# One written order for all five engines, and attention dealt out on a plan of 28 ticks a unit

## The chip, the cores and the metric

The kernel runs on one core of a Trainium2 chip. Time is device microseconds (us) of one execution, and lower is better. The core has five engines, each with a queue of its own: PE (matmul, with PEld for its weight loads), DVE (vector), ACT (activation), POOL (GpSimd) and SP (which issues most DMAs). An engine starts its instructions in the order in which they stand in its queue; an instruction whose input is not ready, or whose output buffer is still in use, holds up all that stand behind it.

## The reference

A block of a transformer with 2048 tokens of width 448: the input, plus a causal attention in four segments with a carried memory, plus a gated feed-forward.

```python
xn = _layernorm(x, axis=-1)
return x + _A_ref(xn, ...) + _B_ref(xn, ...)
# _A_ref: 16 heads of 28, four segments of 512 tokens
logits = jnp.einsum("bhqd,bhkd->bhqk", qs, ks) * scale + mask
p = _softmax(logits, axis=-1)
a_dot = jnp.einsum("bhqk,bhkd->bhqd", p, vs)
o = g * a_mem + (1.0 - g) * a_dot      # a_mem: phi(q) on the memory of the earlier segments
...
# _B_ref: 448 -> 1792 twice, and back
h = _sigmoid(g) * u
return jnp.einsum("bsf,fd->bsd", h, w_down)
```

## The kernel before, in words

**Precision.** Operands are split into a high part (a rounded fp32r copy, made by ACT) and a low part (the remainder, made by DVE). A product is the sum of three partial products, so that one 128x512 result of the feed-forward takes 11 matmuls (`TERMS`), and a projection back six.

**Front.** The first 150 us or so: layer norm, transposes, queries, keys, values and the segment memories. It stands under a schedule of its own (`FRONT`) and the change does not touch it.

**Loop.** Then two streams share the engines.

- *Feed-forward* (`gated`): for each pair of 128-wide slices f, and each of four token blocks b, four slots. A slot is one run of 11 matmuls into `pgu`: side 0 (gate) into a bank tagged `gu`, side 1 (up) into a bank tagged `p`. After side 1, ACT takes tanh of the gate side (`sg`, "the tanh copy"), DVE multiplies it with the up side, ACT makes the high half of `hh`, DVE the low half. Each slot also takes one item off a list of `down` products: six matmuls into `pd`, and an addition to `acc` by DVE. `pd` of odd t shares the two `gu` banks with the gate side, so that two consecutive gate sides get the same bank: **the next gate run on PE cannot start before the tanh copy of the one before it**. New weights (`wgu`, `wdn`, later `wo`) are split by ACT and DVE at fixed slots (`ahead`).
- *Attention*: 32 pairs of heads, two pairs to a unit, 16 units. A pair has five scores (`st`, two PSUM banks tagged `s`), each copied to `w` by ACT and masked by POOL (`affine_select`). Three of them are followed by a maximum on DVE (`mx`). The maxima are joined in short steps that go between DVE and POOL (`up`, `top`), spread by a DVE transpose (`mb`), and then in three parts subtracted from `w` on DVE and put through Exp on ACT. When both pairs of a unit are done, 32 small matmuls form `pa` ("the sums"), and DVE transposes, divides and transposes back, and POOL stores the result to `od`.

**What sets the order.** The code yields at many points. The loop at the end advances attention by one step whenever the feed-forward's steps have gone far enough (n_att attention steps in all, spread evenly between `LEAD` and `TAIL`). Before, attention has 14 steps to a unit (`SLOT`): a score in 10 of them, the sums of the previous unit in step 7, and the later stages of a pair queued one per step behind its scores (`PARTS`). Only PE and SP keep the order of the source (`MANUAL`); on ACT, DVE and POOL the compiler's list scheduler chooses an order from its own cost estimates.

**Tail.** After the feed-forward, `project` splits the attention results (`sums`, loaded from `od`) into `xs`, high by ACT and low by DVE, and multiplies with `wo` (11 matmuls into `po`, 16 times), while the last `down` products are worked off.

The lines of the steps that follow are: `pgu` L247, tanh copy L255, product L256, `hh` L258 and L259, `pd` L173 and L174, weight splits L85 and L86, score L612, its copy L616 and L619, mask L627, maxima L629 and L633, joins L643 to L653, `mb` L656, subtraction L666, Exp L667, sums L687, `xs` splits L753, L102 and L103, `po` L771. In the changed kernel they are L249, L257, L258, L261 and L264, L175 and L177, L87 and L88, L621, L625 and L628, L636, L643 and L647, L656 to L668, L671, L685, L689, L707, L786, L104 and L105, L804.

Of the kernel before, what the change touches and what calls it, by code (L numbers as in the profile page):

```python
# [9 lines left out]
F32 = mybir.dt.float32  # L10
F32R = mybir.dt.float32r
AF = mybir.ActivationFunctionType
ALU = mybir.AluOpType
# [48 lines left out]
def kernel(  # L62
# [103 lines left out]
    def gated():  # L166

        def down(b, hs, wd, t, tag="pd"):
            tok = slice(t * P, (t + 1) * P)
            mms = [(h[:, a, tok], wd[f][:, w, :]) for f, h in hs for a, w in ((0, 0), (0, 1), (1, 0))]  # L170
            pd = bank("pd", tag)
            for n, (l, r) in enumerate(mms):
                T.matmul(pd[:, :D], l, r, start=n == 0, stop=n == len(mms) - 1)  # L173
            V.tensor_add(acc[b][:, t, :], pd[:, :D], acc[b][:, t, :])  # L174
            yield  # L175
            yield

        raw_up, raw_down, wgu, wdn = {}, {}, {}, {}
# [37 lines left out]
        for f0 in range(0, NF, FG):  # L216
# [22 lines left out]
            for b in range(NB):  # L239
                hs = []  # L240
                for f in range(f0, f0 + FG):
                    pgu = []
                    for side in range(2):
                        slot = 2 * (f - f0) + side
                        dst = bank("pgu", ("gu", "p")[side])
                        for n, (a, w) in enumerate(TERMS):
                            T.matmul(dst, wgu[f][:, w, side * P:(side + 1) * P], xs[b][:, a, :],  # L247
                                     start=n == 0, stop=n == len(TERMS) - 1)
                            if n in (3, 7) and f0 + b == 0:  # L249
                                yield  # L250
                        pgu.append(dst)
                        if side == 1:

                            sg = two_k("sg")
                            A.activation(sg, pgu[0], AF.Tanh, scale=0.5)  # L255
                            V.scalar_tensor_tensor(sg, sg, 1.0, pgu[1], op0=ALU.add, op1=ALU.mult)  # L256
                            hh = four_k(F32R, "hh")  # L257
                            A.activation(hh[:, 0, :], sg, AF.Copy, scale=0.5)  # L258
                            V.scalar_tensor_tensor(hh[:, 1, :], sg, 0.5, hh[:, 0, :].bitcast(F32),  # L259
                                                   op0=ALU.mult, op1=ALU.subtract)  # L260
# [322 lines left out]
    class Pair:  # L583
# [16 lines left out]
            at = HW * h + KB[kb]  # L600
            return self.w[:, at:at + w]

        def scores(self):

            self.w = sb.tile([P, 2 * HW], F32, name="w", bufs=3)
            w3 = self.w.rearrange("p (h n) -> p h n", h=2)
            mx = sb.tile([P, 80], F32, name="mx", bufs=2)
            for n in range(5):
                st = bank("st", "s")
                for h, kb in (((n // 2, 0),), ((n // 2, 1), (n // 2, 3)))[n % 2] if n < 4 else ((0, 2), (1, 2)):  # L610
                    at = KB[kb] % L + (256 * h if kb == 2 else 0)
                    T.matmul(st[:, at:at + L - kb * P], self.qk[:KS, 1, h, kb * P:(kb + 1) * P],  # L612
                             self.qk[:KS, 0, h, kb * P:], start=True, stop=True)
                if n < 4:
                    w = self.w[:, HW * (n // 2) + L * (n % 2):][:, :L]
                    A.activation(w, st, AF.Copy)  # L616
                else:
                    w = w3[:, :, 2 * L:]
                    A.activation(w, st.rearrange("p (h n) -> p h n", h=2), AF.Copy)  # L619

                if n % 2 == 0 and n < 4:  # L621
                    d = w[:, :P]
                    pattern = [[1, P]]
                else:
                    d = w.rearrange("p (a n) -> p a n", n=P)[:, 0:4:3, :] if n < 4 else w[:, :, :P]  # L625
                    pattern = [[0, 2], [1, P]]
                G.affine_select(d, d, pattern=pattern, base=0, channel_multiplier=-1, compare_op=ALU.is_ge, fill=MASK)  # L627
                if n in (1, 3):  # L628
                    V.tensor_reduce(mx[:, 16 * (n - 1):16 * (n + 1)],  # L629
                                    w3[:, n // 2, :2 * L].rearrange("p (b n) -> p b n", n=32),  # L630
                                    axis=mybir.AxisListType.X, op=ALU.max, apply_transpose=True)
                if n == 4:
                    V.tensor_reduce(mx[:, 64:80].rearrange("p (h b) -> p h b", h=2),  # L633
                                    w.rearrange("p h (b n) -> p h b n", n=32),
                                    axis=mybir.AxisListType.X, op=ALU.max, apply_transpose=True)
                yield  # L636
            yield from self.weights(mx)

        def weights(self, mx):

            m = mx[:, :64].rearrange("p (h n) -> p h n", h=2)
            m0 = m[:, :, 0:16]
            V.tensor_max(m0[:, :, 4:16], m0[:, :, 4:16], m[:, :, 16:28])  # L643
            V.tensor_max(m0[:, :, 12:16], m0[:, :, 12:16], m[:, :, 28:32])
            V.tensor_max(m0[:, :, 8:16], m0[:, :, 8:16], mx[:, 64:80].rearrange("p (h n) -> p h n", h=2))
            up = sb.tile([P, 2, 16], F32, name="up")
            top = sb.tile([P, 2, 16], F32, name="top")  # L647
            G.tensor_copy(up[0:64], m0[64:128])
            V.tensor_max(m0[0:64], m0[0:64], up[0:64])
            G.tensor_copy(up[0:32], m0[32:64])  # L650
            V.tensor_max(top[0:32], m0[0:32], up[0:32])
            G.tensor_copy(top[32:64], top[0:32])
            G.tensor_copy(top[64:128], top[0:64])  # L653
            yield
            mb = sb.tile([P, 2, L], F32, name="mb")
            V.transpose(mb.rearrange("p h (b n) -> p (h b) n", n=32),  # L656
                        top.rearrange("p h b -> p (h b)").unsqueeze(2).to_broadcast([P, 32, 32]))
            yield
# [3 lines left out]
            quarters = mb.rearrange("p h (b n) -> p h b n", n=P)  # L662
            for w, m in ((w3[:, :, :L], mb),
                         (rest[:, :, :, P:], mb[:, :, 2 * P:].unsqueeze(2).to_broadcast([P, 2, 2, 2 * P])),
                         (rest[:, :, :, :P], quarters[:, :, 1::2, :])):
                V.tensor_sub(w, w, m)  # L666
                A.activation(w, w, AF.Exp, scale=SCALE)  # L667
                yield  # L668

    class Unit:  # L670

# [8 lines left out]

        def finish(self):

            s, i = self.s, self.i
            pa = bank("pa", "m")
            for kb in range(NT):  # L685
                for j in range(HG):
                    T.matmul(pa[32 * j:32 * j + 32, kb * P:], self.vv[:, kb, 32 * j:32 * j + 32],  # L687
                             self.pairs[j // 2].block(j % 2, kb), start=kb == 0, stop=kb == NT - 1)
            on, oc = (self.pairs[1].w[:, n * L:(n + 1) * L] for n in range(2))  # L689
            V.transpose(on, pa)  # L690
            yield
            weigh(sb, on, gate_n[:, i:i + 1], 0.0)
            V.transpose(oc, on)
            nc.gpsimd.dma_start(od[s][P * i:P * (i + 1)], oc, accum_op=ALU.add if s > 0 else ALU.bypass)
            yield
# [4 lines left out]
    def attention():  # L700
# [1 line left out]
            pairs[n].load()  # L702
        units[0].load_values()
        yield
        run, behind, fin = {}, [], None
        for u in range(len(units) + 1):
            for n in range(2):  # L707
                run[n] = pairs[2 * u + n].scores() if u < len(units) else iter(())
            for k, which in enumerate(SLOT):
                if u == len(units):  # L710

                    if k > 9:
                        break
                    which = ((None,) * 8 + (2, None))[k]
                if behind:
                    next(behind.pop(0))
                if fin:
                    next(fin)
                    fin = None
                if which is not None and which < 2 and u < len(units):  # L720
                    next(run[which])
                    n = 2 * u + which + 2
                    if which not in SLOT[k + 1:]:
                        behind += [run[which]] * PARTS
                        if n < len(pairs):
                            pairs[n].load()
                        else:
                            load_sums(n - len(pairs))
                if which == 2 and u > 0:
                    fin = units[u - 1].finish()  # L730
                    next(fin)
                    if u < len(units):
                        units[u].load_values()
                yield

    sums = {}

# [100 lines left out]
```

## Time and profile before

| | |
|---|---|
| median of 3 runs | 687.23 us (687.1 to 687.6) |
| the profiled execution | 687.17 us, span 685.5 us |
| PE busy | 680.3 us, 99% of the span |
| PEld busy | 566.1 us, 83% |
| DVE busy | 567.1 us, 83% |
| ACT busy | 341.6 us, 50% |
| POOL busy | 146.6 us, 21% |
| granted PE clock | 1.00 in every stretch of 50 us |

The span leaves out 1.67 us that lie around it. The prediction shows the lines that carry its argument. In a timeline the columns are start, length, engine, line, operation, out<-in, shapes and count, and in brackets the idle time before it and what ended it. The length of the last matmul of a row is modelled, so rows overlap; the difference of two starts is what a row really took. "84x384 f32 x2" is a short score of 384 and 128 columns; "84x256 f32 x2" has twice 256. In a list of groups the columns are count, busy time and the mean of one in ns, and the idle time before it.

### The profile page before, as it was taken

The numbers are of one execution on the slowest core, as the hardware profiler recorded it, in microseconds if no ns is written. First come the engines' busy times: TensorE is split into PE (matmuls) and PEld (weight loads), VectorE is DVE, ScalarE is ACT, GpSimd is POOL, SyncE is SP. The second block draws the span as 40 slices with busy tenths as digits, with TensorE's granted clock in tenths as the row PEclk, the third lists the DMA queues.
The fourth block names the chain that finished last, engine by engine and source line by source line (L and its number), as shares of the span: only waits on it lengthen the run. The fifth ranks groups of instructions, "written<-read, shape, count | busy, mean of one in ns | idle before, by whom it ended". The sixth has DMA issues, their size and how long they took to land.

```text
span 685.5 us, 10454 instructions
## 1 busy us (share of the span) xinstructions
PE 680.3 (99%) x3594; PEld 566.1 (83%) x3594; DVE 567.1 (83%) x995; ACT 341.6 (50%) x563; POOL 146.6 (21%) x349
## 2 busy tenths in 40 slices
PE   8999999999999999999999999999999999999998
PEld 7898878778878787887878778787887878778897
DVE  6765695767789998988998889988998899889863
ACT  4837555343554455544556446455643465446220
POOL 3500010101223232222232222222322313212000
PEclk9999999999999999999999999999999999999999
DMA  7446556697232333243324243324342423423352
GB/s 268 178 153 232 205 205 245 244 336 182 71 95 76 95 88 86 57 126 80 90 59 107 62 126 72 99 57 117 81 99 73 97 56 83 94 77 96 92 156 107
DMA packets 45940, 84.37 MB, mean 123 GB/s; under 512 B 6336, under 2 KB 20544, under 8 KB 45376
## 3 DMA queue, kind: packets, MB, share of 16 engines
q1 hardware_dynamic: 42736, 76.26, 36.2%
q0 software_dynamic: 3008, 7.34, 5.1%
q8 instruction: 28, 0.46, 0.3%
q14 instruction: 24, 0.20, 0.1%
q10 hardware_dynamic: 144, 0.11, 0.0%
HBM read 51.05 MB, written 32.64 MB: 122 GB/s over the span
## 4 chain that ended last, share of the span: by engine, by line
PE 96%; DMA 1%; SPq 1%; DVE 1%; issue 0%; ACT 0%; DVEq 0%; ACTq 0%
PE pgu L247 41%; PE pd L173 20%; PE pp L355 10%; PE st L612 6%; PE po L771 5%; PE pa L687 5%; PE pv L335 5%; PE pmm L383 2%; PE n L401 2%; DMA acc<-in_x 1%; SPq L747 1%; PE pt L95 1%; PE pk L375 1%; DMA vv<-vd 0%; DVE stats L294 0%
## 5 line engine op out<-in xcount | busy, mean ns | idle before, releaser
L247 PE MATMUL pgu<-xs,wgu 128*128 128x512 f32 x1232 | 303.6, 393 | 0.0
L247 PEld LDWEIGHTS pgu<-xs,wgu 128*128 128x128 f32 x1232 | 228.2, 188 | 46.9 <-issue 2.4
L173 PE MATMUL pd<-wdn,hh 128*128 128x448 f32 x672 | 155.9, 367 | 0.0
L173 PEld LDWEIGHTS pd<-wdn,hh 128*128 128x128 f32 x672 | 122.4, 188 | 12.0 <-issue 0.8
L627 POOL TENSOR_SCALAR_AFFINE_SELECT w<-w 128x256 f32<-128x256 f32 (+1 forms) x160 | 79.7, 501 | 242.0 <-ACT w L616 193.1
L667 ACT ACTIVATE w<-w 128x1024 f32<-128x1024 f32 (+1 forms) x96 | 87.3, 915 | 87.3 <-DVE w L666 86.8
L666 DVE TENSOR_TENSOR w<-w,mb 128x1024 f32<-128x1024 f32 (+1 forms) x96 | 98.7, 1036 | 0.2
L616 ACT ACTIVATE w<-st 128x512 f32<-128x512 f32 x128 | 74.6, 590 | 43.5 <-PE st L612 43.2
L629 DVE TRANSPOSE_TENSOR_REDUCE mx<-w 128x32 f32<-128x1024 f32 x64 | 78.8, 1231 | 14.9 <-POOL w L627 14.9
L355 PE MATMUL pp<-xs,wqk 128*128 128x512 f32 x308 | 77.7, 401 | 0.0
L174 DVE TENSOR_TENSOR acc<-pd,acc 128x448 f32<-128x448 f32 x112 | 67.2, 600 | 1.1 <-PE pd L173 1.1
L355 PEld LDWEIGHTS pp<-xs,wqk 128*128 128x128 f32 x308 | 56.8, 188 | 13.4 <-issue 2.4
L612 PE MATMUL st<-qk 84*128 84x128 f32 (+3 forms) x256 | 62.2, 312 | 0.1
L258 ACT ACTIVATE hh<-sg 128x512 fp32r<-128x512 f32 x56 | 35.2, 628 | 52.5 <-DVE sg L256 41.9
L612 PEld LDWEIGHTS st<-qk 84*128 84x128 f32 x256 | 47.6, 189 | 7.4 <-ACT w L616 0.6
L255 ACT ACTIVATE sg<-pgu 128x512 f32<-128x512 f32 x56 | 33.1, 591 | 37.5 <-PE pgu L247 37.4
L656 DVE STREAM_TRANSPOSE mb<-top 128x1024 f32<-128x1024 f32 x32 | 39.7, 1242 | 12.5 <-POOL top L653 12.2
L362 DVE TENSOR_TENSOR qk<-pp,qk 128x512 fp32r<-128x512 f32 x28 | 19.3, 688 | 29.8 <-ACT e L360 23.7
L259 DVE SCALAR_TENSOR_TENSOR hh<-sg,hh 128x512 fp32r<-128x512 f32 x56 | 38.9, 694 | 2.8 <-ACT hh L258 2.4
L335 PE MATMUL pv<-wv,xs 128*128 128x448 f32 x176 | 39.7, 376 | 0.2
L256 DVE SCALAR_TENSOR_TENSOR sg<-sg,pgu 128x512 f32<-128x512 f32 x56 | 37.4, 667 | 1.8 <-PE pgu L247 1.6
L687 PE MATMUL pa<-w,vv 128*32 128x128 f32 (+3 forms) x512 | 37.9, 436 | 0.0
(100 smaller groups left out, 640.7 us busy)
## 6 DMA issues: line engine op xcount, KB each, us to landing
qk<-qd SPq DMA_DIRECT2D x192, 112.0 KB
qd<-qk SPq DMA_DIRECT2D x28, 512.0 KB
raw<-in_w_ffn SPq DMA_DIRECT2D x14, 512.0 KB
vd<-vst SPq DMA_DIRECT2D x4, 1024.0 KB
vv<-vd SPq DMA_DIRECT2D x16, 256.0 KB
od<-w POOLq DMA_DIRECT2D x16, 256.0 KB, 4.0
sums<-od SPq DMA_DIRECT2D x32, 128.0 KB
out<-acc SPq DMA_DIRECT2D x15, 224.0 KB
```

The source lines that it names most:

```text
L173: T.matmul(pd[:, :D], l, r, start=n == 0, stop=n == len(mms) - 1)
L174: V.tensor_add(acc[b][:, t, :], pd[:, :D], acc[b][:, t, :])
L247: T.matmul(dst, wgu[f][:, w, side * P:(side + 1) * P], xs[b][:, a, :], start=n == 0, stop=n == len(TERMS) - 1)
L335: T.matmul(pv[:, :D], xs[b][:, a, t * P:(t + 1) * P], wv[w], start=n == 0, stop=n == len(TERMS) - 1)
L355: T.matmul(pp, wqk[c][:, w, :], xs[b][:, a, :], start=n == 0, stop=n == len(TERMS) - 1)
L612: T.matmul(st[:, at:at + L - kb * P], self.qk[:KS, 1, h, kb * P:(kb + 1) * P], self.qk[:KS, 0, h, kb * P:], start=True, stop=True)
L616: A.activation(w, st, AF.Copy)
L627: G.affine_select(d, d, pattern=pattern, base=0, channel_multiplier=-1, compare_op=ALU.is_ge, fill=MASK)
L629: V.tensor_reduce(mx[:, 16 * (n - 1):16 * (n + 1)], w3[:, n // 2, :2 * L].rearrange("p (b n) -> p b n", n=32), axis=mybir.AxisListType.X, ...
L666: V.tensor_sub(w, w, m)
L667: A.activation(w, w, AF.Exp, scale=SCALE)
L687: T.matmul(pa[32 * j:32 * j + 32, kb * P:], self.vv[:, kb, 32 * j:32 * j + 32], self.pairs[j // 2].block(j % 2, kb), start=kb == 0, stop=k ...
```

## The change

All five engines now keep the order of the source in the loop (`MANUAL`). Attention is a plan: 28 ticks to a unit, and each stage of a pair is put at a tick of its own: the scores at `SCORES` (counted from the unit's start, first and second pair), each maximum two ticks after its score, the four join steps 3 to 6 ticks after the last score, the three subtractions 8, 9 and 10 ticks after it, each Exp one tick after its subtraction, the sums at tick 14 of the next unit and their later stages 2, 4, 5 and 6 ticks after that. Within a tick the work is sorted by a rank (scores 0, sums and Exp 1, loads 2, maxima 3, joins 4, subtractions 5, the sums' later stages 6). The five scores of a pair come in another order, so that the last one, at tick 14, is a short one (384 and 128 columns) that directly precedes the sums. In the feed-forward the tanh copy, the high half and the low half are separated by yields, and the addition of a `down` product comes one yield after its matmuls. What is computed is unchanged.

```diff
-SLOT = (0, 0, 0, None, 0, 0, None, 2, 1, 1, 1, None, 1, 1)
-PARTS = 5
+TICKS = 28
+SCORES = ((2, 4, 8, 10, 14), (16, 18, 20, 24, 26))
+SUMS, END = 14, 21
...
-MANUAL = {mybir.EngineType.PE, mybir.EngineType.SP}
+MANUAL = {mybir.EngineType.PE, mybir.EngineType.SP, mybir.EngineType.Activation, mybir.EngineType.DVE,
+          mybir.EngineType.Pool}
...
+            yield
             V.tensor_add(acc[b][:, t, :], pd[:, :D], acc[b][:, t, :])
-            yield
             yield
...
                             A.activation(sg, pgu[0], AF.Tanh, scale=0.5)
                             V.scalar_tensor_tensor(sg, sg, 1.0, pgu[1], op0=ALU.add, op1=ALU.mult)
+                            yield
                             hh = four_k(F32R, "hh")
                             A.activation(hh[:, 0, :], sg, AF.Copy, scale=0.5)
+                            if f0 + b > 0:
+                                yield
                             V.scalar_tensor_tensor(hh[:, 1, :], sg, 0.5, hh[:, 0, :].bitcast(F32),
                                                    op0=ALU.mult, op1=ALU.subtract)
                             hs.append((f, hh))
-                        for _ in range(1 if f0 + b == 0 else 3):
-                            yield
+                            if f0 + b > 0:
+                                yield
+                        else:
+                            for _ in range(1 if f0 + b == 0 else 3):
+                                yield
...
+        for n, pair in enumerate(pairs):
+            first = TICKS * (n // 2)
+            ticks = [first + tick for tick in SCORES[n % 2]]
+            for k, tick in enumerate(ticks):
+                at(tick, 0, pair.score, k)
+                if k > 1:
+                    at(tick + 2, 3, pair.maximum, k)
+            at(ticks[-1], 2, following, n + 2)
+            for k, late in enumerate((3, 4, 5, 6)):
+                at(ticks[-1] + late, 4, pair.join, k)
+            for k in range(3):
+                at(ticks[-1] + 8 + k, 5, pair.subtract, k)
+                at(ticks[-1] + 9 + k, 1, pair.exponents, k)
+        for u, unit in enumerate(units):
+            tick = TICKS * (u + 1) + SUMS
+            at(tick, 1, unit.finish)
+            if u + 1 < len(units):
+                at(tick, 2, units[u + 1].load_values)
+            for late, work in ((2, unit.back), (4, unit.divide), (5, unit.turn), (6, unit.store)):
+                at(tick + late, 6, work)
+        for work in plan:
+            for _, run, args in sorted(work, key=lambda w: w[0]):
+                run(*args)
+            yield
...
-    n_att = len(units) * len(SLOT) + 10
+    n_att = len(units) * TICKS + END
```

**Place 1, PE, the sums inside unit 8 (counting from 0; those of unit 7).** `xs_68` is token block 3. Before:

```order
L247 MATMUL pgu<-xs_68,wgu 128x512 x11
L173 MATMUL pd<-wdn,hh 128x448 x6
L687 MATMUL pa<-w,vv 32x512 x4
L687 MATMUL pa<-w,vv 32x384 x4
L687 MATMUL pa<-w,vv 32x256 x4
L687 MATMUL pa<-w,vv 32x128 x4
L247 MATMUL pgu<-xs_68,wgu 128x512 x11
```

In the changed kernel a short score, of 384 and of 128 columns, stands between `pd` and the sums:

```order
L249 MATMUL pgu<-xs_68,wgu 128x512 x11
L175 MATMUL pd<-wdn,hh 128x448 x6
L621 MATMUL st<-qk_3976 128x384
L621 MATMUL st<-qk_3976 128x128
L707 MATMUL pa<-w,vv 32x512 x4
L707 MATMUL pa<-w,vv 32x384 x4
L707 MATMUL pa<-w,vv 32x256 x4
L707 MATMUL pa<-w,vv 32x128 x4
L249 MATMUL pgu<-xs_68,wgu 128x512 x11
```

In 15 of the 16 units the sums now follow a short score, which none did before.

**Place 2, ACT, the same unit a few us later.** `w_4150` (before) and `w_4145` (now) are the scores of unit 8's first pair, `sg_4403` and `sg_4409` the tanh copy of slice 7 in block 3, `wgu_4388` and `wgu_4394` the weights of slice 9. Before:

```order
L255 ACTIVATE sg_4321<-pgu_4256 128x512
L667 ACTIVATE w_4150<-w_4150 128x2x512
L616 ACTIVATE w_4334<-st_4336 128x512
L667 ACTIVATE w_4150<-w_4150 128x2x2x256
L258 ACTIVATE hh_4324<-sg_4321 128x512
L616 ACTIVATE w_4334<-st_4352 128x512
L85 ACTIVATE wgu_4388<-raw_3815 128x1024
L255 ACTIVATE sg_4403<-pgu_4360 128x512
```

And now:

```order
L257 ACTIVATE sg_4306<-pgu_4240 128x512
L625 ACTIVATE w_4309<-st_4311 128x512
L261 ACTIVATE hh_4319<-sg_4306 128x512
L625 ACTIVATE w_4309<-st_4328 128x512
L628 ACTIVATE w_4309<-st_4363 128x2x256
L689 ACTIVATE w_4145<-w_4145 128x2x512
L625 ACTIVATE w_4309<-st_4385 128x512
L689 ACTIVATE w_4145<-w_4145 128x2x2x256
L87 ACTIVATE wgu_4394<-raw_3815 128x1024
L257 ACTIVATE sg_4409<-pgu_4351 128x512
```

Both large Exps of the pair stand ahead of this tanh copy in both, but they moved from right behind the previous tanh copy to right in front of this one, past three copies of scores and a half of `hh`.

**Place 3, ACT, the end of the loop.** `xs0_65` is the split of the attention result that `po` multiplies first, `hh_6521` (before) the high half of the third feed-forward result from the end, `hh_6678` (now) that of the last. Before:

```order
L667 ACTIVATE w_6308<-w_6308 128x2x512
L616 ACTIVATE w_6498<-st_6500 128x512
L753 ACTIVATE xs0_65<-sums_6421 128x4x128 x3
L667 ACTIVATE w_6308<-w_6308 128x2x2x256
L258 ACTIVATE hh_6521<-sg_6518 128x512
```

And now:

```order
L689 ACTIVATE w_6468<-w_6468 128x2x512
L689 ACTIVATE w_6468<-w_6468 128x2x2x256
L87 ACTIVATE wo_6659<-raw_6099 128x896
L257 ACTIVATE sg_6674<-pgu_6634 128x512
L689 ACTIVATE w_6468<-w_6468 128x2x2x128
L261 ACTIVATE hh_6678<-sg_6674 128x512
L786 ACTIVATE xs0_65<-sums_6445 128x4x128 x4
```

Before, three of the four splits of block 0 stood two feed-forward slices ahead of the end; now all stand behind the last half of `hh`. On DVE the low part of the first split before:

```order
L666 TENSOR_TENSOR w_6308<-w_6308,mb_6461 128x2x2x128
L259 SCALAR_TENSOR_TENSOR hh_6521<-sg_6518,hh_6521 128x512
L174 TENSOR_TENSOR acc1_70<-pd_6542,acc1_70 128x448
L629 TENSOR_REDUCE mx_6499<-w_6498 128x32
L102 TENSOR_TENSOR xs0_65<-sums_6421,xs0_65 128x3x128
L103 TENSOR_TENSOR xs0_65<-sums_6421,xs0_65 64x128
```

And now:

```order
L88 TENSOR_TENSOR wo_6659<-raw_6099,wo_6659 128x896
L258 SCALAR_TENSOR_TENSOR sg_6674<-sg_6674,pgu_6662 128x512
L264 SCALAR_TENSOR_TENSOR hh_6678<-sg_6674,hh_6678 128x512
L177 TENSOR_TENSOR acc2_71<-pd_6681,acc2_71 128x448
L104 TENSOR_TENSOR xs0_65<-sums_6445,xs0_65 128x3x128
```

It moved from among the maxima of the last pair to behind the last product, half and addition of the loop.

More of the change, by code (lines that the diff above doesn't have):

```diff
@@ L601, in block, with score @@
             return self.w[:, at:at + w]
-        def scores(self):
-            self.w = sb.tile([P, 2 * HW], F32, name="w", bufs=3)
+        def score(self, n):
+            if n == 0:
+                self.w = sb.tile([P, 2 * HW], F32, name="w", bufs=3)
+                self.mx = sb.tile([P, 80], F32, name="mx", bufs=2)
             w3 = self.w.rearrange("p (h n) -> p h n", h=2)
[L607 to L637, printed above, removed]
@@ L670, with subtract, exponents @@
+        def subtract(self, n):
+            w, m = self.part(n)
+            V.tensor_sub(w, w, m)
+        def exponents(self, n):
+            w, _ = self.part(n)
+            A.activation(w, w, AF.Exp, scale=SCALE)
     class Unit:
@@ L688, in finish, with back, divide, turn @@
                              self.pairs[j // 2].block(j % 2, kb), start=kb == 0, stop=kb == NT - 1)
[L689 to L695, printed above, removed]
+            self.pa = pa
+            self.on, self.oc = (self.pairs[1].w[:, n * L:(n + 1) * L] for n in range(2))
+        def back(self):
+            V.transpose(self.on, self.pa)
+        def divide(self):
+            weigh(sb, self.on, gate_n[:, self.i:self.i + 1], 0.0)
+        def turn(self):
+            V.transpose(self.oc, self.on)
+        def store(self):
+            s, i = self.s, self.i
+            nc.gpsimd.dma_start(od[s][P * i:P * (i + 1)], self.oc, accum_op=ALU.add if s > 0 else ALU.bypass)
     pairs = [Pair(n) for n in range(NB * H // 2)]
@@ L704, in attention @@
         yield
[L705 to L734, printed above, removed]
@@ new lines, in attention, with at, following @@
+        plan = [[] for _ in range(n_att + 1)]
+        def at(tick, rank, work, *args):
+            plan[tick].append((rank, work, args))
+        def following(n):
+            if n < len(pairs):
+                pairs[n].load()
+            else:
+                load_sums(n - len(pairs))
+        for n, pair in enumerate(pairs):
[11 more added lines that the diff above has]
+                at(ticks[-1] + 9 + k, 1, pair.exponents, k)
```

81 lines of the change are left out of this document (55 added, 26 removed).

## The prediction

> **What bounds the kernel now.** I read the page's busy times and its chain first, then PE's timeline, then the waits of DVE, then ACT and DVE at one place.
>
> ```profile
> PE 680.3 (99%) x3594; PEld 566.1 (83%) x3594; DVE 567.1 (83%) x995; ACT 341.6 (50%) x563; POOL 146.6 (21%) x349
> PE 96%; DMA 1%; SPq 1%; DVE 1%; issue 0%; ACT 0%; DVEq 0%; ACTq 0%
> ```
>
> PE is busy for 99% of the span and carries 96% of the chain. Here are 16 us of its timeline (start, length, operation):
>
> ```profile
> 376.26 2.65 PE L247 MATMUL pgu<-xs,wgu 128*128 128x512 f32 x11
> 378.84 2.36 PE L687 MATMUL pa<-w,vv 128*32 128x512 f32 x32
> 381.13 1.47 PE L173 MATMUL pd<-wdn,hh 128*128 128x448 f32 x6
> 382.44 0.40 PE L612 MATMUL st<-qk 84*128 84x512 f32 x1
> 382.68 2.67 PE L247 MATMUL pgu<-xs,wgu 128*128 128x512 f32 x11
> 385.18 0.40 PE L612 MATMUL st<-qk 84*128 84x384 f32 x2
> 385.42 1.42 PE L173 MATMUL pd<-wdn,hh 128*128 128x448 f32 x6
> 386.67 0.40 PE L612 MATMUL st<-qk 84*128 84x512 f32 x1
> 386.91 2.66 PE L247 MATMUL pgu<-xs,wgu 128*128 128x512 f32 x11
> 389.40 1.37 PE L173 MATMUL pd<-wdn,hh 128*128 128x448 f32 x6
> 390.61 0.40 PE L612 MATMUL st<-qk 84*128 84x384 f32 x2
> 390.85 2.75 PE L247 MATMUL pgu<-xs,wgu 128*128 128x512 f32 x11
> 393.44 0.40 PE L612 MATMUL st<-qk 84*128 84x256 f32 x2
> ```
>
> From start to start a run of 11 costs 2.49 to 2.50 us (382.68, 386.91), `pd` 1.21 (389.40), a score 0.24, the sums 2.29. What differs is set by the neighbours: a run costs 2.59 behind a short score (390.85) and 2.58 ahead of the sums (376.26), `pd` 1.25 behind a short score (385.42) and 1.31 behind the sums (381.13). Nothing else varies, so PE doesn't wait here, and **every wait that the change brings to PE lengthens the kernel**, while removing waits elsewhere gains nothing.
>
> [...]
>
> DVE is next:
>
> ```profile
> 200.00:600.00 400.00, 400.00 (x2174) 327.40 (x2173) 361.07 (x584) 209.86 (x332) 105.29 (x260) 1.00 0.34 87
> DVE mx L629 <- POOL w L627: 11.0, 17, 1.7
> DVE mb L656 <- POOL top L653: 9.9, 18, 0.6
> ```
>
> In the loop DVE is busy for 361.1 of 400 us; 20.9 of the 38.9 idle us are these two waits for POOL. With joins a tick apart most of them should go. That is spare time for DVE, not for PE.
>
> **The change part by part.** *The front, and what is computed,* stay as they are: 0.
>
> *PE's neighbours.* I counted the pairs of blocks in both orders. Short scores ahead of a run fall from 26 to 21, ahead of `pd` from 29 to 26, ahead of another score from 9 to 2, and 15 now stand ahead of the sums. At 0.10, 0.04 and 0.04 (an estimate for the last, like `pd`) that is 0.5 + 0.1 + 0.3 = 0.9 us gained. No row shows the sums behind a short score. If its price and the sums' 0.09 hide in each other, 15 x 0.09 = 1.35 more is gained: -2.2. If both stay, 15 x 0.10 = 1.5 is lost: +0.6. I take -0.9, near the middle: the sums' own 0.09 stays, and the short score's price goes.
>
> *Stages given out apart.* This moves the subtractions and Exps. The first pair's scores end at tick 14 instead of about 10, and its three subtractions come at ticks 22, 23 and 24 instead of steps that began at ticks 16, 18 and 20. All three, and their Exps, now fall into three neighbouring ticks, behind the busiest stretch of DVE. Before, at the place that the order shows on ACT (place 2), the first subtraction started 3.0 us after the sums (407.48 + 2.29 = 409.77):
>
> ```profile
> 407.48 2.36 PE L687 MATMUL pa<-w,vv 128*32 128x512 f32 x32
> 412.74 1.19 DVE L666 TENSOR_TENSOR w<-w,mb 128x1024 f32<-128x1024 f32 x1
> 413.84 0.24 DVE L135 RECIPROCAL rc<-w 128x16 f32<-128x16 f32 x1
> 414.02 1.06 ACT L667 ACTIVATE w<-w 128x1024 f32<-128x1024 f32 x1 [6.10 <-DVE w L666]
> 414.98 0.58 ACT L616 ACTIVATE w<-st 128x512 f32<-128x512 f32 x1
> 415.46 1.05 ACT L667 ACTIVATE w<-w 128x1024 f32<-128x1024 f32 x1
> 416.41 0.61 ACT L258 ACTIVATE hh<-sg 128x512 fp32r<-128x512 f32 x1
> ...
> 417.40 1.05 ACT L85 ACTIVATE wgu<-raw 128x1024 fp32r<-128x1024 f32 x1
> 418.36 0.59 ACT L255 ACTIVATE sg<-pgu 128x512 f32<-128x512 f32 x1
> 422.34 2.01 PE L247 MATMUL pgu<-xs,wgu 128*128 128x512 f32 x8
> ```
>
> Start to start, an Exp took 0.96 us, a copy 0.48, the weight split 0.96; a DVE instruction overlaps the next by 0.09 (1.19 against 1.10), and ACT started 0.09 after DVE's subtraction ended (413.93). The tanh copy (418.36) was over at 418.95, 3.4 us before the run that needs its bank (422.34). Now the same place in the new order, with these DVE means:
>
> ```profile
> L629 DVE TRANSPOSE_TENSOR_REDUCE mx<-w 128x32 f32<-128x1024 f32 x55 | 67.6, 1230 | 11.0 <-POOL w L627 11.0
> L666 DVE TENSOR_TENSOR w<-w,mb 128x1024 f32<-128x1024 f32 x54 | 64.6, 1202 | 0.1
> L174 DVE TENSOR_TENSOR acc<-pd,acc 128x448 f32<-128x448 f32 x89 | 53.3, 599 | 0.0
> L656 DVE STREAM_TRANSPOSE mb<-top 128x1024 f32<-128x1024 f32 x27 | 33.5, 1242 | 10.3 <-POOL top L653 9.9
> L259 DVE SCALAR_TENSOR_TENSOR hh<-sg,hh 128x512 fp32r<-128x512 f32 x45 | 31.3, 695 | 2.0 <-ACT hh L258 1.7
> L256 DVE SCALAR_TENSOR_TENSOR sg<-sg,pgu 128x512 f32<-128x512 f32 x44 | 29.3, 666 | 0.7 <-PE pgu L247 0.7
> L633 DVE TRANSPOSE_TENSOR_REDUCE mx<-w 128x16 f32<-128x512 f32 x28 | 19.4, 694 | 1.0 <-POOL w L627 1.0
> L645 DVE TENSOR_TENSOR mx<-mx 128x16 f32<-128x16 f32 x27 | 4.8, 177 | 0.6
> ```
>
> Count from the end of the run behind the sums, where DVE has caught up (the sums give it 2.3 us). DVE then has, in order: product 0.67, maximum 1.23, `pa` back 0.69 (as L633), three small maxima 0.53, low half 0.70, small 0.18, reciprocal 0.18 and weighing 0.69 (as L645 and L633), small 0.18, turning 0.69, addition 0.60, `mb` 1.24, maximum 0.69, subtraction 1.20: 9.5 less 14 overlaps of 0.09, so the first subtraction ends at 8.2 to 8.4 and the second at 9.5. ACT: Exp from 8.5 to 9.4, a copy to 9.9, Exp to 10.9, weight split to 11.8, tanh copy to 12.4. PE: two scores 0.48, `pd` 1.22, run 2.50, score 0.24, `pd` 1.21, score 0.24, run 2.59, score 0.24, `pd` 1.25 = 10.0, and wants the bank. **It waits 2.4 us.**
>
> From the end of its side-1 run a tanh copy has 1.45 to 1.7 us (one `pd`, one or two scores), 4 where the sums come between. I carried the same sum along the whole order (DVE's backlog grows by what stands in its queue and shrinks by PE's time) and found nine of the 56 copies too late behind Exps: 2.4, 1.5, 1.4, 1.3, 1.0, 0.9, 0.3, 0.2 and 0.1, together 9.1 us. If DVE gets there 1 us sooner (no wait left for POOL), 1.4 + 0.5 + 0.4 + 0.3 = 2.6 remain; if 1 us later (DVE waiting in its turn for ACT's late halves), 9 more and some 2 from copies now just in time, an estimate: 20. I take 9.1, because the waits for POOL that go and those for ACT that come have about the same size.
>
> *The other consequences of the order* cost nothing as long as the backlog, at most 6 us in that sum, stays below what they allow: additions (a bank of `pd` comes round after two slots, 9 us), `hh` (three slots, 13 us, before `pd` reads it), the sums (last subtraction 1.6 to 5 us ahead), qk loads on SP (issued at tick 14 and 26, 16 and 18 ticks ahead of use), the store behind `turn` on POOL (next mask four ticks later). Loads of `vv` still stand behind the qk loads on SP.
>
> *The end of the loop* (place 3). Before, splits for `po` ran early:
>
> ```profile
> 633.12 1.15 ACT L753 ACTIVATE xs<-sums 128x512 fp32r<-128x512 f32 x2 [0.32 <-DMA sums<-od]
> 636.88 2.36 PE L771 MATMUL po<-wo,xs 128*128 128x448 f32 x11
> L102 DVE TENSOR_TENSOR xs<-sums,xs 128x384 fp32r<-128x384 f32 x16 | 9.0, 561 | 2.6 <-ACT xs L753 1.6 <-DMA out<-acc 0.9
> ```
>
> Two splits started 3.8 us ahead of the first `po`. Now they stand last. From the end T of the last run: the backlog puts the second Exp's end at T+0.35; `wo` high (7/8 of 1.05, an estimate) to 1.2, tanh copy to 1.8; DVE's `wo` low (7/8 of 1.20) to 2.35, product to 3.0; ACT's high half to 3.7, `xs` to 4.2; DVE's low half to 4.4, addition to 4.9, `xs` low (0.56) to 5.5. PE wants this for `po`'s third matmul at T + 1.21 + 0.4. **It waits 4.0 us**, and full as PE is to the end, nothing wins that back. With both engines caught up the chain is still 0.67 + 0.6 + 0.6 + 0.5 + 0.56 and five hand-overs of 0.09, 3.4: +1.8 at least. With another Exp in front: +4.6.
>
> **Sum.** 687.17 - 0.9 + 9.1 + 4.0 = 699.4 us, made against the profiled execution, 0.06 below the median.
>
> **The rivals.**
> - *Only the end pays.* DVE, freed from POOL, is always early enough: 687.2 - 0.9 + 4.0 = 690.3. For it, the 20.9 us of waits; against it, that in the worked place no POOL wait is counted. 16%.
> - *DVE becomes the bound.* Its idle time is 38.9 in 400 us, 2.8 a unit of 28.6 us (378.84 to 407.48). If waiting for late tanh copies and halves takes 4, each of 16 units loses 1.2 on top of the end's 4 and some of the nine places: about 710. 6%.
> - *PE absorbs the waits.* If PE could run faster after a late start than its 2.49 us a run, lost time would be caught up in the runs behind it: 687.2 - 0.9 = 686.3. The constant runs speak against it, and for it only that weight loads fill 83%. [...] 4%.
> - *Faster.* The short score at the sums hides both prices, 15 x 0.15, and the chain at the end is overtaken: 687.2 - 2.2 = 685.0. It decides only if all waits together stay below 0.8 us, less than half of the end's least price. 4%.
>
> **How the numbers follow.** Both costs paid, 699.4, has 70%, with a range of its own from 693 to 705. About 0.2% is what a measurement of this kernel can tell from no change. The range from 690 to 706 holds the first rival and the likeliest case but for its ends; it leaves out the bound by DVE, the two fast cases, and the upper end of 20 + 4.6. Faster 4%, within 0.2% 4% (PE absorbs), slower 92%.
>
> **What would show it.** PE idle or stretched runs ahead of gate runs, released by the tanh copy, in about nine places, most of them one or two slots behind Exps; a gap of 2 to 4.5 us at the first `po`, released by `xs` on DVE; short waits of DVE for POOL mostly gone; the Exp of each first pair 8 to 9 us behind the sums instead of 4; runs of 2.49 us unchanged; the run ahead of the sums back at 2.49. Wrong would be: no gap at the first `po`; DVE's subtractions earlier than I count; waits at scores or sums instead.

## The result, and the profile after

The changed kernel takes 725.63 us (median of four runs, 722.53 to 727.46) against 687.16 us before (686.98 to 687.60): a ratio of 1.0554, 95% interval 1.0514 to 1.0595. It is slower by 38.5 us. The prediction was slower by 12.2, to 699.4, at most 706: the direction was right, the size was not.

The busy times and the chain of the page of the changed kernel:

```profile
PE 695.0 (96%) x3594; PEld 573.1 (79%) x3594; DVE 572.7 (79%) x995; ACT 338.2 (47%) x563; POOL 137.5 (19%) x349
PE 61%; DVE 20%; ACT 8%; issue 7%; POOL 2%; DMA 1%; SPq 0%; POOLq 0%; DVEq 0%; ACTq 0%
```

PE carries 61% of the chain where it carried 96%: followed back from its last instruction, the chain now passes again and again through DVE and ACT. PE's busy time has grown as well, by 14.7 us, although its 3594 matmuls are the same. The waits of PE (who waits, for whom, us in total, times, longest):

```profile
PE pgu L249 <- ACT sg L257: 19.7, 11, 3.0
PE po L804 <- ACT xs L786: 5.2, 1, 5.2
...
PE st L621 <- ACT w L625: 0.3, 1, 0.3
```

Eleven gate runs wait for the tanh copy of the gate run before, and the first `po` waits for its split. Both are what the prediction named. The timeline of the place that it worked out, inside unit 8 (PE, DVE and ACT):

```profile
427.41 0.62 PE L621 MATMUL st<-qk 84*128 84x512 f32 x2
427.68 0.69 DVE L258 SCALAR_TENSOR_TENSOR sg<-sg,pgu 128x512 f32<-128x512 f32 x1 [3.33 <-PE pgu L249]
...
433.06 0.40 PE L621 MATMUL st<-qk 84*128 84x384 f32 x2
...
435.31 2.32 DVE L685 TENSOR_TENSOR w<-w,mb 128x1024 f32<-128x1024 f32 x2
...
436.12 1.42 PE L175 MATMUL pd<-wdn,hh 128*128 128x448 f32 x6
436.58 1.06 ACT L689 ACTIVATE w<-w 128x1024 f32<-128x1024 f32 x1 [3.94 <-DVE w L685]
...
437.55 0.58 ACT L625 ACTIVATE w<-st 128x512 f32<-128x512 f32 x1
438.02 1.05 ACT L689 ACTIVATE w<-w 128x1024 f32<-128x1024 f32 x1
...
438.97 1.05 ACT L87 ACTIVATE wgu<-raw 128x1024 fp32r<-128x1024 f32 x1
439.91 0.59 ACT L257 ACTIVATE sg<-pgu 128x512 f32<-128x512 f32 x1
...
440.55 4.38 PE L249 MATMUL pgu<-xs,wgu 128*128 128x512 f32 x11 [3.02 <-ACT sg L257]
...
444.77 0.40 PE L621 MATMUL st<-qk 84*128 84x512 f32 x1
```

The run behind the sums ends at 427.41. ACT sits idle for 3.94 us in front of the first Exp, because DVE has not finished the subtraction; then copy, Exp and weight split go first, and the tanh copy that PE needs comes last. (The copy at 437.55 is that of the score of 433.06, over by 433.46: it stood for 4.1 us behind the Exp in ACT's queue.) PE is through with `pd` at 437.33 and waits until 440.55. The row of 440.55 shows something else: the run behind the wait takes 4.22 us (440.55 to 444.77) instead of 2.50. The same two things at the next large wait, PE first, then the windows (length; busy time of PE, PEld, DVE, ACT and POOL; granted PE clock; DMA):

```profile
512.40 1.42 PE L175 MATMUL pd<-wdn,hh 128*128 128x448 f32 x6
516.81 5.06 PE L249 MATMUL pgu<-xs,wgu 128*128 128x512 f32 x11 [3.00 <-ACT sg L257]
521.67 0.63 PE L621 MATMUL st<-qk 84*128 84x384 f32 x2
```

```profile
500.00:512.00 12.00, 12.00 (x58) 10.37 (x57) 9.98 (x17) 5.46 (x9) 2.39 (x8) 1.00 0.21 57
512.00:517.00 5.00, 2.00 (x11) 1.54 (x10) 3.20 (x5) 4.68 (x7) 0.41 (x1) 0.87 0.00 0
517.00:522.00 5.00, 5.00 (x13) 3.94 (x13) 4.63 (x7) 1.34 (x3) 0.48 (x1) 0.50 0.01 3
```

From 517 to 522, behind a wait of 3.00 us, PE's granted clock is 0.50, and the 11 matmuls of the run take 4.86 us (516.81 to 521.67). This term was not in the prediction at all.

Start to start along PE's whole timeline, the 40.3 us by which the span has grown (725.8 against 685.5) come from: 21.8 at the eleven gate runs (the waits, and 0.2 at each restart, as in the worked place: 3.22 from 437.33 to 440.55, of which 3.02 are listed as a wait); 5.4 at the first `po`; 9.1 in five runs of 3.6 to 4.9 us behind such waits and the scores and sums after them; 2.6 in the `po` and sums behind the end's gap; 0.5 at a score. The remaining 0.9 is small waits, less what PE's new neighbours save.

### The profile page after: what moved, and what is told of

Its sections match the earlier page's. It is cut to its first block, busy times and chain, and to the rows that moved or that the text cites. A ratio compares the mean times of both kernels' runs of the same rounds, so it can differ in the third digit from the quotient of the medians.

```text
span 725.8 us, 10527 instructions
## 1 busy us (share of the span) xinstructions
PE 695.0 (96%) x3594; PEld 573.1 (79%) x3594; DVE 572.7 (79%) x995; ACT 338.2 (47%) x563; POOL 137.5 (19%) x349
## 4 chain that ended last, share of the span: by engine, by line
PE 61%; DVE 20%; ACT 8%; issue 7%; POOL 2%; DMA 1%; SPq 0%; POOLq 0%; DVEq 0%; ACTq 0%
PE pgu L249 22%; PE pp L363 10%; PE pd L175 9%; PE po L804 5%; PE pa L707 4%; ACT w L689 4%; PE pv L343 4%; DVE w L685 4%; DVE mx L643 3%; PE st L621 3%; DVE mb L671 2%; DVE acc L177 2%; DVE sg L258 2%; PE pmm L391 1%; PE n L409 1%
## 5 line engine op out<-in xcount | busy, mean ns | idle before, releaser
L249 PE MATMUL pgu<-xs,wgu 128*128 128x512 f32 x1232 | 311.6, 402 | 19.8 <-ACT sg L257 19.7
L249 PEld LDWEIGHTS pgu<-xs,wgu 128*128 128x128 f32 x1232 | 232.2, 192 | 72.4 <-ACT sg L257 24.6
L689 ACT ACTIVATE w<-w 128x1024 f32<-128x1024 f32 (+1 forms) x96 | 85.2, 912 | 102.6 <-DVE w L685 101.8
L175 PEld LDWEIGHTS pd<-wdn,hh 128*128 128x128 f32 x672 | 123.2, 189 | 12.2 <-issue 0.8
L636 POOL TENSOR_SCALAR_AFFINE_SELECT w<-w 128x256 f32<-128x256 f32 (+1 forms) x160 | 68.3, 427 | 295.9 <-ACT w L625 213.1
L685 DVE TENSOR_TENSOR w<-w,mb 128x1024 f32<-128x1024 f32 (+1 forms) x96 | 96.5, 1036 | 0.2
L258 DVE SCALAR_TENSOR_TENSOR sg<-sg,pgu 128x512 f32<-128x512 f32 x56 | 37.9, 677 | 19.9 <-PE pgu L249 12.9
L804 PE MATMUL po<-wo,xs 128*128 128x448 f32 x176 | 37.9, 370 | 5.3 <-ACT xs L786 5.2
L707 PE MATMUL pa<-w,vv 128*32 128x256 f32 (+3 forms) x512 | 40.2, 452 | 0.0
L804 PEld LDWEIGHTS po<-wo,xs 128*128 128x128 f32 x176 | 33.2, 190 | 8.6 <-ACT xs L786 5.6
```

The source lines that it names most:

```text
L804: T.matmul(po[:, :D], xs[b][:, a, t * P:(t + 1) * P], out_weights(w), start=m == 0, stop=m == len(TERMS) - 1)
```

## The experiments

**Which part of the change costs.** The change does two separable things: it sets up a plan for attention, and it keeps the written order on three more engines. First the plan alone, with ACT, DVE and POOL ordered by the scheduler again:

```diff
-MANUAL = {mybir.EngineType.PE, mybir.EngineType.SP, mybir.EngineType.Activation, mybir.EngineType.DVE,
-          mybir.EngineType.Pool}
+MANUAL = {mybir.EngineType.PE, mybir.EngineType.SP}
```

> The plan of 28 ticks and the new score order stay, but ACT, DVE and POOL are ordered by the list scheduler again, as before the change. If the written order on ACT (tanh copies and splits behind late Exps) is the cause, the waits ahead of gate runs and of po go, and the time is 687 to 692 us. If the plan itself, which gives DVE its subtractions late, is the cause, most of the 25 us of waits stay and the time is 710 us or more.

Measured: 692.57 us, ratio to before 1.008 (1.0063 to 1.0097). The eleven waits and the one at `po` are gone, and the clock is 1.00. What is left is that sums wait for Exps:

```profile
PE pa L706 <- ACT w L688: 3.2, 2, 2.5
```

Start to start its 16 sums take 43.4 us, before 36.8: 6.6 more, of which the last unit's sums make 4.4. (The list of waits has only 3.2 of it; another 3.3 is in the busy time of the sums, 41.2 us against 37.9 before.) With ACT alone left to the scheduler, DVE and POOL in written order (`Activation` taken out of `MANUAL`):

> The changed kernel, but ACT alone is ordered by the list scheduler again; DVE and POOL keep the written order. If ACT's written order is what costs, the time is that of the kernel with all three ordered by the scheduler (692.6 us) within 4 us. If DVE's written order costs as much by itself, it is over 705.

Measured: 697.24 us (1.0133 to 1.0164), 0.7 outside the 4 us, far from 705. The waits of PE are these:

```profile
PE po L804 <- DVE xs L104: 4.4, 1, 4.4
...
PE pa L707 <- ACT w L689: 1.3, 3, 0.5
```

So the written order of DVE and POOL costs 4.7 us on top of the plan, and the row that it adds is the 4.4 at the first `po`; ACT's written order costs 28.4, from 697.24 to 725.63. In this run DVE, with the same order, does 360.3 us of work in the 400 us from 200 to 600, while PE is busy for 398.6 of them: DVE isn't the bound. The other way round, the written order alone, on the old steps:

```diff
-MANUAL = {mybir.EngineType.PE, mybir.EngineType.SP}
+MANUAL = {mybir.EngineType.PE, mybir.EngineType.SP, mybir.EngineType.Activation, mybir.EngineType.DVE,
+          mybir.EngineType.Pool}
```

> The kernel before, with its own 14 steps a unit, but all five engines in the order of its source. If a written order is harmful wherever Exps stand ahead of tanh copies, it is slower than before by 10 us or more (over 697). If only the new plan's places for subtractions and Exps do harm, it stays within 3 us of 687.

Measured: 842.54 us, ratio 1.2263 (1.2245 to 1.2282).

```profile
PE st L613 <- ACT w L617: 65.1, 34, 4.9
PE pgu L248 <- ACT sg L256: 28.2, 16, 4.3
PE po L772 <- ACT xs L754: 6.8, 1, 6.8
```

In the old steps an Exp was written directly behind its subtraction, and ACT stood still there for 226.6 us in all; the score copies behind it held up PE as well. The plan is thus a remedy: the written order costs 155.5 us without it (842.54 against 687.03) and 33 with it (725.63 against 692.57).

**Is it the Exps ahead of the tanh copies?** Each tanh copy is written one run earlier, right behind its gate run:

```diff
                         pgu.append(dst)
+                        if side == 0:
+                            sg = two_k("sg"); A.activation(sg, dst, AF.Tanh, scale=0.5)
                         if side == 1:
-                            sg = two_k("sg")
-                            A.activation(sg, pgu[0], AF.Tanh, scale=0.5)
```

> Each tanh copy is written right behind its gate run instead of behind the side-1 run, one run and a pd earlier, which gives it about 4 us more; all else is the changed kernel. If the late tanh copies make the loop's loss, its 20 us of waits and some 9 us of slow runs behind them go, and the time is 694 to 700 us, with the end's 8 us left. If DVE is the bound, it lags as before and the waits move to scores, sums or side-1 runs: 710 us or more.

Measured: 710.46 us (ratio 1.0331 to 1.0362), at the edge of the second case. No gate run waits, but scores do:

```profile
PE po L804 <- ACT xs L786: 5.0, 1, 5.0
PE st L621 <- ACT w L628: 4.5, 4, 1.8
PE st L621 <- ACT w L625: 3.6, 6, 1.6
```

ACT now stands waiting at tanh copies until the gate run is over (29.6 us in 19 waits from 160 to 680), and the copies of scores come late behind them. The 19.7 us became 8.1 elsewhere. In the other remedy the tanh copy stays and the Exps come later:

```diff
-                at(ticks[-1] + 9 + k, 1, pair.exponents, k)
+                at(ticks[-1] + 12 + k, 1, pair.exponents, k)
```

> One number of the plan: each Exp comes four ticks after its subtraction instead of one; all else is the changed kernel. If tanh copies are late because Exps stand ahead of them on ACT before DVE has finished their subtractions, three ticks (3 us) cover most of DVE's lag: the waits ahead of gate runs fall from 20 us to under 5, and the time is 698 to 706 us, with the end's 8 us left. If DVE as such is too slow for the loop, it stays over 715, or sums wait for Exps instead.

Measured: 712.02 us (1.0341 to 1.0375).

```profile
PE po L804 <- ACT xs L786: 6.2, 1, 6.2
PE pa L707 <- ACT w L689: 5.0, 7, 1.7
```

All eleven waits ahead of gate runs are gone: three ticks were enough, and the Exps that stood ahead of the tanh copies while DVE lagged were their cause. ACT's own waiting for subtractions has fallen from 101.8 to 7.1 us. But the sums now need what comes too late: 54.3 us for the 16 of them instead of 36.8 (the last of them, behind the wait of 6.2 us at `po`, take 4.42 us instead of 2.29). The time fell less than the first theory said, and the second one's "sums wait for Exps instead" holds. On ACT an Exp has two limits, DVE's lag ahead of it and the sums behind it, and neither one tick nor four ticks behind the subtraction keeps both everywhere.

**The stretched matmuls.** Spare matmuls fill PE's waits; they go to the bank of the sums and are never read:

```diff
+FILL = {13: 2, 14: 8, 16: 10, 19: 3, 27: 8, 29: 4, 32: 12, 40: 12, 45: 8, 48: 6}
...
+    def spin(src, count):
+        dm = bank("dm", "m") if count else None
+        for n in range(count):
+            T.matmul(dm, src[:, 0, :P], src[:, 0, :], start=n == 0, stop=n == count - 1)
...
+                        spin(xs[b], 0 if side else FILL.get(4 * f0 + 2 * b + f - f0, 0))
                         dst = bank("pgu", ("gu", "p")[side])
...
+                spin(xs[3], 22 if n == 2 else 0)
                 po = bank("po", ("p", "gu")[n % 2])
```

> The changed kernel with spare matmuls put where its trace shows PE waiting: 2 to 12 of them (0.23 us each, into the bank of the sums, never read) ahead of the ten gate runs that wait longest, and 22 ahead of the first po, each group a little shorter than its wait. The waits for ACT stay as they are, only PE isn't idle in them. If the granted clock falls because PE was idle, the runs behind are back at 2.50 us, the sums and po behind the end's gap too, the clock stays at 1.00, and the time falls by 10 to 13 us, to 713 to 716. If those runs are slow for another reason (DVE or ACT beside them), they stay slow and the time stays within 3 us of 725.6.

Measured: 717.47 us (1.0425 to 1.0456), clock 0.999 where the changed kernel has 0.981. The place of 512.40 to 522, in this kernel:

```profile
509.28 2.88 PE L170 MATMUL dm<-xs 128*128 128x512 f32 x12
512.45 2.79 PE L256 MATMUL pgu<-xs,wgu 128*128 128x512 f32 x11 [0.29 <-ACT sg L264]
515.08 0.40 PE L628 MATMUL st<-qk 84*128 84x384 f32 x2
```

The gate run starts as late as before (3.2 us behind the end of `pd`), and takes 2.63 us. Nothing was gained but the clock: 8.2 us by the medians, 10.0 by the two spans, so somewhat less than the 10 to 13 expected. The four runs lie within 0.15 us of each other; those of the changed kernel spread over 4.9. With half as many spare matmuls in each place (1 to 6, and 11 at the end), part of each wait is idle again:

> As the kernel with spare matmuls in PE's waits (717.5 us), with half as many in each, so that about half of each wait is idle again (1.0 to 1.6 us in the loop, some 2.7 at the end). If the clock falls only after idle stretches of about 2 us or more, the loop's runs stay at 2.50 us and only the end's po and sums are slow: 717 to 720 us. If it falls by the share of idle time whatever the length of a stretch, half of the loss is back: about 721.

Measured: 719.01 us (1.0445 to 1.0476).

```profile
PE pgu L256 <- ACT sg L264: 11.5, 11, 1.7
PE po L812 <- ACT xs L793: 2.7, 1, 2.7
```

No run behind these eleven waits is stretched (2.64 us at most); behind the 2.7 at the end the sums take 3.23 us instead of 2.29. Both are as the first theory said, and so is the time; the last section has a run in which two shorter waits were followed by a stretched one.

**The end.** The first two splits of `xs` are given out in the last slices:

```diff
                 ahead[3, 2] = lambda: ready_out(1)
+                ahead[3, 0] = lambda: split_tokens(0, 0)
+                ahead[3, 1] = lambda: split_tokens(0, 1)
...
                 b, t = divmod(n, NT)
-                split_tokens(b, t)
+                if n >= 2:
+                    split_tokens(b, t)
```

> The first two splits of the attention result into xs stand in the last feed-forward slices instead of behind them; all else is the changed kernel (725.6 us). If the gap ahead of the first po and the slow matmuls right behind it are what the end costs (5.2 + 1.45 + 1.2 us in the trace), the time falls by 7 to 8 us, to about 718, and the first po no longer waits. If the gap is replaced by another one, for the last Exps and sums, the time falls by less than 3 us.

Measured: 723.36 us, 2.3 less than the changed kernel, which is within the 4.9 over which that kernel's runs spread. `po` no longer waits, but the last sums behind it wait for their Exp:

```profile
PE pa L709 <- ACT w L691: 1.9, 1, 1.9
```

This is the second case, a new wait in the old one's place. With both remedies:

> Both remedies together: Exp four ticks after its subtraction (but for the last pair), and the first two splits of xs in the last slices. If the loop's waits and the end's waits are separate and each remedy holds, 687 to 696 us: what is left is the sums' wait for the last Exps, 2 to 4 us. If a third wait takes over, over 700.

Measured: 706.37 us (1.0269 to 1.0299). The third wait took over: sums, 55.7 us for 16.

**Is there an arrangement that keeps the plan?** With the scheduler on ACT, DVE and POOL, the sums come one tick later, the last unit's four ticks later still, and the plan ends five steps of the loop later. The kernel of the first expectation below leaves out the last unit's store to `od`; that of the second, whose edit is shown, has it.

```diff
-LEAD, TAIL = 15, 53
+LEAD, TAIL = 15, 48
...
-SUMS, END = 14, 21
+SUMS, END = 15, 26
...
-            tick = TICKS * (u + 1) + SUMS
+            tick = TICKS * (u + 1) + SUMS + 4 * (u == 15)
```

> The plan with ACT, DVE and POOL ordered by the list scheduler (692.6 us), the sums one tick later, those of the last unit four ticks later still, and the whole plan ending five steps of the loop later. If the plan's own price is that sums wait for the last Exps (6.6 us over all 16 units in that run's trace), most of it goes and the time is 686 to 689 us. If the sums are late for another reason, it stays at 692.

> The plan with ACT, DVE and POOL ordered by the list scheduler, sums one tick later (those of the last unit four more), the plan ending five steps of the loop later, and now one tick more at its end, so that the last unit's store is in it. That store lies off PE's path: 688 to 689 us, 1 to 2 us over the kernel before. If the store or the loads behind it hold up the last po, 690 or more; if nothing of the plan costs anything, 686 to 687.

Measured: 688.70 us without the store, 687.62 with it (ratio 1.0007, 0.9998 to 1.0016), 0.4 below the range that was expected. Its sums take 37.1 us. So most of the 5.5 us of the plan alone were sums and end (moved together here, so not told apart), and the repaired plan can't be told from the kernel before. The same places for the sums with all five engines in written order, with Exps 12 ticks (first pair) and 10 (second) behind the last score instead of 9, and also without the last unit's store:

> All five engines in written order, each Exp four ticks after its subtraction in a unit's first pair and two in its second, the sums as in the kernel beside this one, and the first two splits of xs in the last slices. If an Exp has to stand between two limits on ACT (behind DVE's lag, ahead of the sums), the waits ahead of gate runs stay under 8 us, those of the sums under 3, and the time is 690 to 698 us. If written order costs in any arrangement of Exps, over 703.

Measured: 709.73 us (1.0308 to 1.0339). A miss: six gate runs wait 8.2 us, two of them 2.96 and 2.26 us long with stretched runs behind (4.16 and 4.31 us), and waits of scores for their copies, of `po` for the split of `wo` and of sums come to 5.1 more. No kernel with ACT in written order came under 706.

## Why the prediction was wrong in size

**PE's neighbours, -0.9: right.** A short score ahead of the sums, in the changed kernel:

```profile
643.01 0.40 PE L621 MATMUL st<-qk 84*128 84x384 f32 x2
643.34 2.36 PE L707 MATMUL pa<-w,vv 128*32 128x512 f32 x32
```

It takes 0.33 instead of 0.24: the sums' 0.09 now falls on the score, and the score's own price is gone, which was the value taken. The plan alone, with the scheduler on ACT, DVE and POOL, has the same order of blocks on PE as the changed kernel and no waits ahead of runs: there runs, `pd` and scores take 461.7 us from start to start, and 462.9 before. That is 1.2 less, where 0.9 was forecast.

**Tanh copies, 9.1: the mechanism right, the size wrong.** The worked place went as written, row by row: the bank was wanted at 437.33 (9.9 us behind the run's end, forecast 10.0), and ACT did Exp, copy, Exp, split, tanh. DVE got to the end of the first subtraction 9.1 us behind that run's end, where 8.2 to 8.4 was counted, so PE waited 3.02 instead of 2.4. (The sign "8 to 9 us behind the sums instead of 4" mixed two starting points: the 8 to 9 were counted from the end of the run behind the sums, the 4 from the end of the sums. Counted from the end of the sums, at 424.79, the Exp at 436.58 came 11.8 us behind.) The step that failed is "I take 9.1, because the waits for POOL that go and those for ACT that come have about the same size". They don't. From 200 to 600 us, DVE's waits before, beside the two rows shown in the prediction, and then those after:

```profile
DVE top L651 <- POOL up L650: 6.3, 20, 0.5
DVE mx L649 <- POOL up L648: 5.9, 15, 0.7
DVE hh L259 <- ACT hh L258: 1.7, 3, 1.0
...
DVE sg L256 <- PE pgu L247: 0.7, 1, 0.7
```

```profile
DVE sg L258 <- PE pgu L249: 11.3, 5, 3.3
DVE mx L643 <- POOL w L636: 10.3, 17, 1.7
DVE wgu L88 <- ACT wgu L87: 7.2, 6, 1.8
DVE sg L258 <- ACT sg L257: 5.7, 7, 1.3
DVE top L666 <- POOL up L664: 5.4, 9, 1.9
DVE mx L663 <- POOL up L661: 5.1, 13, 0.7
DVE mb L671 <- POOL top L668: 4.9, 9, 0.6
DVE hh L264 <- ACT hh L261: 4.8, 8, 0.8
```

Waits for POOL fell from 33.1 us (11.0 + 9.9 + 6.3 + 5.9) to 25.7: "mostly gone" was wrong. Waits for ACT and PE rose from 2.4 to 29.0. So the two did not cancel. DVE in written order waits at its own place for what is late; that it passes this delay on to the Exps is the likely reading, and was not tried by itself. The upper estimate, 20 "if 1 us later", is near what came, 19.7; that DVE was some 1 us later at each place isn't shown.

**The end, 4.0: 5.2.** Behind the last run's end T = 668.17 the sum put the end of the second Exp at T + 0.35:

```profile
668.17 1.38 PE L175 MATMUL pd<-wdn,hh 128*128 128x448 f32 x6
668.76 2.21 ACT L689 ACTIVATE w<-w 128x1024 f32<-128x1024 f32 x2 [5.59 <-DVE w L685]
...
674.10 4.25 ACT L786 ACTIVATE xs<-sums 128x512 fp32r<-128x512 f32 x8
...
674.77 2.32 PE L804 MATMUL po<-wo,xs 128*128 128x448 f32 x4 [5.23 <-ACT xs L786]
```

It ended at T + 2.8: again an Exp waited for DVE's subtractions, for 5.59 us, and the end was put too early by 2.45 us, more than the upper end of 4.6 allowed. The 5.2 is the wait ahead of the first matmul, while the 4.0 was counted to the third, which was wanted at T + 1.6; it started at 675.98, T + 7.8, so by the prediction's own count it was 6.2 us late (the two matmuls before it ran at a granted clock of 0.50). And the wait could not be won back by early splits alone, since the last sums wait close behind it.

**A term was missing: the clock.** "Nothing else varies" was read from a kernel whose PE was busy for 400.00 of the 400 us from 200 to 600. Five of the six waits of 2.01 to 3.02 us ahead of gate runs, and the one of 5.23 at `po`, cost another 1.5 to 2.7 us each in slow matmuls: 11.7 in the trace, 8.2 by the medians of the runs with spare matmuls. Had 19.7, 5.2 and 11.7 stood in the sum, it would have come to 687.2 - 0.9 + 36.6 = 722.9, against 725.63 (727.46 in the execution that was profiled).

**The rivals.** "Only the end pays" fell with the eleven waits; "DVE becomes the bound" with the run in which DVE's order stayed and ACT's went; "PE absorbs the waits" with the constant runs: no run took less than 2.49 us, before or after, though weight loads were busy for only 83% of the span before and 79% after. That this share leaves PE room was not shown. "Faster" fell too; the plan without the written order is at best equal.

What stays open: why DVE was 0.7 to 0.9 us later at the worked place (0.27 of it lies between the run's end and the product, 427.41 to 427.68) and which of DVE's waits made which tanh copy late were not tried; and no run separates the causes of the 709.73 us further.

## What to carry to other kernels

Under a written order, ask of each instruction that the bounding engine waits for what stands ahead of it in its own queue and how late that can be: here one Exp, written one tick behind its subtraction, stood waiting for it for 3.94 us, held up a tanh copy and through it PE, for 3.02 us. Where delays can feed each other, as they seem to here, take the bound in which they add up, not the one in which they cancel. And a wait of a full PE can cost more than its length: here five of six waits of 2.01 to 3.02 us cost another 1.5 to 2.7 us in the matmuls behind them.

## What the runs showed of the hardware that was not expected

In the changed kernel PE's granted clock was lower behind most of the longer waits: five of the six ahead of gate runs from 2.01 to 3.02 us were followed by runs of 3.6 to 4.9 us, whose mean granted clock was 0.50 (behind the wait of 3.00) to 0.70 (behind 2.19). Behind the one of 2.60 us the run took 2.61, at a clock of 1.00, and no run was stretched behind the five waits up to 1.61 us, nor behind the eleven up to 1.7 in the kernel with half as many spare matmuls.

```profile
285.02 2.77 PE L249 MATMUL pgu<-xs,wgu 128*128 128x512 f32 x11 [2.60 <-ACT sg L257]
```

In one place shorter waits had a stretched run behind them: in the kernel before with all five engines in written order, two waits of 1.29 and 0.93 us with a single score between them were followed by a run of 4.18 us (452.11 to 456.29).

```profile
450.68 0.51 PE L613 MATMUL st<-qk 84*128 84x512 f32 x1 [1.29 <-ACT w L617]
452.11 4.34 PE L248 MATMUL pgu<-xs,wgu 128*128 128x512 f32 x11 [0.93 <-ACT sg L256]
```

With PE kept busy by the spare matmuls (11 waits of 0.4 us at most left ahead of gate runs), the runs behind took 2.66 us at most, and the mean granted clock was 0.999 instead of 0.981. Why the wait of 2.60 us was spared, and how the clock is set, no run here shows.
